# Values of later tokens through DRAM, memory slots last, and one attention store per segment, in a recurrent-memory attention kernel

## Chip, cores, metric

One core of one Trainium2 chip. The metric is device time in microseconds (us); lower is better. Before: median 1245.14 us (1236.84 to 1247.9, 4 runs).

## The reference

Attention in 64 segments of 32 tokens. Each segment attends over 8 memory slots and its own tokens; its output for the memory slots is the next segment's memory, so the segments form a chain. A gated feed-forward part follows.

```python
# S = 2048 tokens, Dm = 640, H = 32 heads of Dh = 128, M = 8 slots, seg_len = 32
for s in range(n_seg):
    h = concatenate([mem, x[:, 32 * s:32 * s + 32]], axis=1)          # 8 + 32 rows
    q, k, v = h @ Wq, h @ Wk, h @ Wv
    p = softmax(where(mask, q @ k.T * scale, -1e9))                   # token rows: causal; memory rows: all
    o = (p @ v) @ Wo
    mem = o[:, :M]                                                    # goes to the next segment
    outs.append(o[:, M:])
# then h = x + attention, and h + (relu(gate) * up) @ W_down on its layer norm
```

## The kernel before

TensorE projects 32 rows at a time: the 8 memory rows of segment s and, in the same pass, 24 *riders*, token rows that a later segment will need. Every fourth segment a group of 32 more tokens (`act_e`) is projected in between. The 32 heads lie in four groups g of 32 partitions: partition 32g + t holds row t of group g. The names in the profiles: `act_r` is the input of a pass; `tok` holds projected rows before their transpose; `Qr`, `KS` and `Kr` are the queries and keys that the scores read; `Vp` holds the values of the pass just projected, `Vr` those gathered for a segment's own tokens; `oT` is the attention output before the output projection, `wtok` the finished attention rows; `Pbd` holds the probabilities of the memory rows and, for `woe`, attention rows on their way out. Four features of this kernel matter here.

**1. A recorder derives all waits.** `add` notes what each operation reads and writes; a wait is made for each conflict of keys. All DMAs below are issued by SyncE, in program order: a DMA whose inputs aren't ready holds up all DMAs behind it (in the changed kernel's class 1 stretches, defined below, the inputs of KS are written by 9.9 us and KS is issued at 14.8, behind stores that wait; means of 14).

```python
def dma(dst, src, r=(), w=(), eng="sp"):
    add(eng, lambda e: e.dma_start(dst, src), r=r, w=w, dma=True)
```

**2. K goes through a DMA transpose every segment** (`KS<-tok`, and `Kr<-tok` for the 32 extra tokens of every fourth). The score matmuls wait for it.

```python
project(a, ks, 1, (0,), (P2,)); to_tok(P2, 0, "act")      # K, first half of the heads
project(a, ks, 1, (1,), (P3,)); to_tok(P3, 1, "dve")      # K, second half
dma_t(KS..., tokp[0][:, :], [("tok", 0), ("tok", 1)], [("KS",)])
# ... pv_x(s - 1), Q and V projections, evictions ...
scores(s)                                                 # reads KS, Kr, Qr
```

**3. The riders' values are moved by many small copies**, since tokens that sit at row 8 and up of their pass must sit at other rows in their own segment:

```python
def v_riders(par, t0, n):                                 # 4 or 8 copies of 8, 16 or 24 rows
    done = 0
    while done < n:
        t = t0 + done
        q, o = seg_slot(t // SEG), t % SEG
        m = min(n - done, SEG - o)
        for g in range(4):
            a = 32 * g + M + done
            dma(Vr[q][32 * g + o:32 * g + o + m, :, :], Vp[par][a:a + m, :, :], ...)
        done += m
```

**4. Attention rows are stored in four pieces a segment**, and the last 8 tokens of four segments, computed together (`woe`), in eight:

```python
def store_attn(src, skey, p0, t0, n):
    for g in range(4):
        dma(attn_d[t0:t0 + n, g, :], src[32 * g + p0:32 * g + p0 + n, :, :]..., r=[skey], w=[("attn", t0, g)])

def woe_store(b):                                         # where s % 4 == 1
    for j in range(4):
        for dg in range(2):
            t0 = 32 * (4 * b + j)
            dma(attn_d[t0:t0 + M, 2 * dg:2 * dg + 2, :]..., ap(Pbd, ...), r=[("Pbd", 0), ("Pbd", 1)], w=[("attn", t0, dg)])
# ... in the segment loop, after the scores: v_riders, pv_mem, wo_pass, store_attn, [Kr transpose], [woe_store]
```

The softmax here doesn't subtract the row's maximum and nothing guards it: scores larger than these inputs give would overflow.

## Time and profile before

I cut the trace at the first score matmul of each segment and call a segment's number modulo 4 its class: class 1 has the `woe` work and its stores, class 2 the Kr transpose. A stretch runs from the scores of one segment to those of the next, so what a class issues delays the scores at the end of its stretch.

| mean of 12 segments, us | class 0 | class 1 | class 2 | class 3 |
|---|---|---|---|---|
| length of the stretch | 14.69 | 16.43 | 16.01 | 15.74 |
| PE idle in it | 0.77 | 2.24 | 1.56 | 1.30 |

The loop from the second to the last scores takes 972.0 us, 94 of them with PE idle; the opening takes 38.7 and the feed-forward part 200.9 us.

Here are lines of the page of the kernel before: busy time by engine, then two groups (line, engine, operation, out<-in, count, busy us, mean ns, idle before it and what ended most of that).

```profile
PE 1114.9 (90%) x30140; PEld 577.0 (46%) x27792; DVE 564.4 (45%) x1438; ACT 333.2 (27%) x684; POOL 25.3 (2%) x92
...
L369 PE MATMUL ps<-ident,tok 128*128 128x128 bf16 x664 | 51.2, 220 | 17.9 <-DVE tok L378 13.3
...
L484 PE MATMUL ps<-Qr,Kr 128*32 128x40 bf16 x2048 | 41.9, 186 | 25.2 <-DMA KS<-tok 25.0
```

TensorE is the limit, but it stands 25.2 us before score matmuls, nearly all of it for the transpose of KS. The waits of the same kernel (who waited for whom: us in total, times, longest) show the second late transpose:

```profile
ACT tok L376 <- DMA Kr<-tok: 54.7, 12, 5.1
PE ps L484 <- DMA KS<-tok: 25.0, 16, 3.0
DVE tok L378 <- DMA Kr<-tok: 22.2, 12, 2.5
PE ps L369 <- DVE tok L378: 13.3, 11, 1.5
```

The Q evictions write the buffer that the Kr transpose reads, so they wait until it has landed, and PE's transposes of Q wait for them. Why the transposes are late is to be read from SyncE's timeline (start us, us, operation, out<-in, count), here a stretch of class 1 and the next of class 2:

```profile
636.28 6.34 SPq L306 DMA_DIRECT2D Vr<-Vp  x8
642.67 2.95 SPq L306 DMA_DIRECT2D attn_d<-wtok  x4
645.67 2.66 SPq L306 DMA_DIRECT2D attn_d<-Pbd  x8
648.43 1.26 SPq L309 DMA_TRANSPOSE KS<-tok  x1
...
652.78 5.72 SPq L306 DMA_DIRECT2D Vr<-Vp  x8
658.55 1.68 SPq L306 DMA_DIRECT2D attn_d<-wtok  x4
660.33 1.82 SPq L309 DMA_TRANSPOSE Kr<-tok  x1
```

The queue has no break: 12 us of issuing small copies, and only then KS, 3.6 us after its input was ready. In the mean SyncE issues for 14.2 of the 16.4 us of a class 1 stretch.

### The profile page before, as it was taken

The numbers are of one execution on the slowest core, as the hardware profiler recorded it, in microseconds if no ns is written. First come the engines' busy times: TensorE is split into PE (matmuls) and PEld (weight loads), VectorE is DVE, ScalarE is ACT, GpSimd is POOL, SyncE is SP. The second block draws the span as 40 slices with busy tenths as digits, with TensorE's granted clock in tenths as the row PEclk, the third lists the DMA queues.
The fourth block names the chain that finished last, engine by engine and source line by source line (L and its number), as shares of the span: only waits on it lengthen the run. The fifth ranks groups of instructions, "written<-read, shape, count | busy, mean of one in ns | idle before, by whom it ended". The sixth has DMA issues, their size and how long they took to land.

```text
span 1245.2 us, 62156 instructions
## 1 busy us (share of the span) xinstructions
PE 1114.9 (90%) x30140; PEld 577.0 (46%) x27792; DVE 564.4 (45%) x1438; ACT 333.2 (27%) x684; POOL 25.3 (2%) x92
## 2 busy tenths in 40 slices
PE   5589999989899989989988989999989986999998
PEld 2344445444445544544444544454445454533443
DVE  3244545444444444554544544454445442443522
ACT  2123223322232222232322222233223321211311
POOL 1000000000000000000000000000000000000000
PEclk9889999999999999999999999999999998999999
DMA  9933333324343334343434344423242329121200
GB/s 360 337 53 68 58 67 59 66 57 67 56 66 59 70 57 66 60 81 66 79 70 81 66 82 64 65 55 79 42 78 57 63 58 323 27 80 27 69 22 22
DMA packets 218274, 102.12 MB, mean 82 GB/s; under 512 B 190688, under 2 KB 206752, under 8 KB 218016
## 3 DMA queue, kind: packets, MB, share of 16 engines
q1 hardware_dynamic: 217824, 98.13, 36.8%
q8 instruction: 227, 3.72, 1.3%
q14 instruction: 31, 0.25, 0.1%
q10 hardware_dynamic: 192, 0.01, 0.0%
HBM read 36.79 MB, written 6.55 MB: 35 GB/s over the span
## 4 chain that ended last, share of the span: by engine, by line
PE 77%; DMA 11%; DVE 6%; SPq 3%; issue 3%; ACT 1%; DVEq 0%
PE ps L350 27%; PE ps L541 13%; PE ps L336 10%; PE ps L883 10%; DMA KS<-tok 5%; DMA Kr<-tok 3%; SPq L306 3%; PE ps L484 3%; PE ps L369 3%; PE ps L916 3%; PE ps L578 3%; PE ps L553 2%; DMA Wo<-in_A_Wo_dram 2%; PE ps L517 2%; DVE TBf L465 2%
## 5 line engine op out<-in xcount | busy, mean ns | idle before, releaser
L350 PE MATMUL ps<-W,act_r 128*32 128x512 bf16 x6640 | 456.5, 385 | 27.7 <-DVE act_r L466 12.7
L350 PEld LDWEIGHTS ps<-W,act_r 128*32 128x32 bf16 x6640 | 170.0, 97 | 275.4 <-issue 74.3
L541 PE MATMUL ps<-Wo,oT 128*32 128x160 bf16 x8448 | 165.3, 236 | 35.2 <-DVE oT L378 23.8
L378 DVE CAST tok<-ps 128x512 bf16<-128x512 f32 x161 | 111.1, 690 | 151.6 <-PE ps L350 97.3
L541 PEld LDWEIGHTS ps<-Wo,oT 128*32 128x32 bf16 x8448 | 149.1, 98 | 49.5 <-DVE oT L378 35.5
L376 ACT ACTIVATE tok<-ps 128x512 bf16<-128x512 f32 x161 | 95.9, 596 | 249.9 <-PE ps L336 134.6
L336 PE MATMUL ps<-W,act_r 128*32 128x512 bf16 x1240 | 120.6, 379 | 0.3 <-issue 0.3
L376 ACT ACTIVATE wtok<-ps 128x160 bf16<-128x160 f32 x64 | 19.5, 304 | 311.4 <-DVE TBf L465 302.3
L465 DVE STREAM_TRANSPOSE TBf<-ps 128x160 f32<-128x160 f32 x64 | 22.4, 350 | 174.6 <-PE ps L541 174.6
L350 PE MATMUL ps<-W,act_e 128*32 128x512 bf16 x900 | 94.2, 395 | 1.5 <-issue 1.5
L336 PE MATMUL ps<-W,act_e 128*32 128x512 bf16 x900 | 93.3, 392 | 0.8 <-issue 0.8
L591 DVE TENSOR_TENSOR ox<-ps,rx 128x512 bf16<-128x512 f32 x128 | 82.5, 686 | 2.2
L376 ACT ACTIVATE Qr<-ps 128x768 bf16<-128x768 bf16 (+3 forms) x110 | 69.2, 658 | 42.0 <-DVE Qr L378 26.7
L369 PE MATMUL ps<-ident,tok 128*128 128x128 bf16 x664 | 51.2, 220 | 17.9 <-DVE tok L378 13.3
L883 PE MATMUL ps<-xn2T,Wg 128*128 128x512 bf16 x260 | 65.6, 383 | 0.0
L883 PE MATMUL ps<-xn2T,Wu 128*128 128x512 bf16 x260 | 65.5, 383 | 0.0
L484 PE MATMUL ps<-Qr,Kr 128*32 128x40 bf16 x2048 | 41.9, 186 | 25.2 <-DMA KS<-tok 25.0
L898 DVE TENSOR_TENSOR hT<-g,ps 128x512 bf16<-128x512 bf16 (+1 forms) x56 | 38.5, 688 | 57.1 <-PE ps L883 53.3
L916 PE MATMUL ps<-Wd,hT 128*128 128x320 bf16 (+1 forms) x240 | 63.3, 300 | 0.0
L369 PEld LDWEIGHTS ps<-ident,tok 128*128 128x128 bf16 x664 | 37.4, 98 | 52.8 <-DVE tok L378 48.0
L378 DVE CAST Vp<-ps 128x512 bf16<-128x512 f32 x64 | 44.1, 689 | 33.1 <-PE ps L350 33.1
L896 ACT ACTIVATE g<-ps 128x512 bf16<-128x512 f32 (+1 forms) x56 | 32.5, 593 | 95.9 <-PE ps L883 95.9
(82 smaller groups left out, 1006.1 us busy)
## 6 DMA issues: line engine op xcount, KB each, us to landing
Vr<-Vp SPq DMA_DIRECT2D x124, 48.8 KB
W<-in_A_Wk_dram SPq DMA_DIRECT2D x2, 2560.0 KB
W<-in_A_Wq_dram SPq DMA_DIRECT2D x2, 2560.0 KB
W<-in_A_Wv_dram SPq DMA_DIRECT2D x2, 2560.0 KB
Wo<-in_A_Wo_dram SPq DMA_DIRECT2D x2, 2560.0 KB
xt<-in_A_x_dram SPq DMA_DIRECT2D x30, 160.0 KB
Vr<-Vp SPq DMA_DIRECT2D x128, 32.5 KB
attn_d<-wtok SPq DMA_DIRECT2D x256, 7.5 KB
```

Source lines behind the costliest of these rows:

```text
L336: return pe.add_instruction(mybir.InstMatmult(name=nc.get_next_instruction_name(), engine=mybir.EngineType.PE, ins=[pe.lower_ap(rhs), pe.l ...
L350: ins = pe.matmul(*a, start=(c == 0), stop=(c == DC - 1), skip_group_check=True)
L369: ins = pe.matmul(bank_bf(b)[:, k * 128:(k + 1) * 128], t[:, (k % 4) * 128:(k % 4 + 1) * 128], ident[:, :], is_transpose=True)
L376: add("act", lambda a: a.activation(dst, src, ACTF.Copy), r=r, w=w)
L378: add("dve", lambda v: v.tensor_copy(dst, src), r=r, w=w)
L465: add("dve", lambda v: v.transpose(TBf[:].rearrange("p c t -> p (c t)"), src), r=[wkey], w=[("TBf",)])
L484: i = pe.matmul(o, lh, Qr[:, h, q, :], start=True, stop=True, skip_group_check=True)
L541: i = pe.matmul(bank(bk)[32 * gg:32 * gg + 32, 0:160], src[:, hb, :], w[:, gg], start=(hb == 0), stop=(hb == 31), skip_group_check=True)
L591: add("dve", lambda v, kh=kh: v.tensor_tensor(ox[:, kh, :, :], src[:, :, kh, 0:128], ap(rx, kh, [[2, 4], [0, 128]]), ALU.mult), r=[B(b0 + ...
L883: ins = pe.matmul(bank(bk), w[:, c, lo:lo + 128], xn2T[par][:, c, :], start=(c == 0), stop=(c == DC - 1))
L898: add("dve", lambda v: v.tensor_tensor(hT[par][lo:128, j, :], g1[gi][lo:128, :], bank(bu)[lo:128, :], ALU.mult), r=[B(bu), ("g1", gi)], w= ...
L916: i = pe.matmul(*a, start=(j == 0), stop=(j == FC - 1), skip_group_check=True)
```

## The change

Intent: take most of those issues off SyncE. All rows of a pass are stored to a DRAM table by token number in one DMA (`v_store`), and the next segment's 32 rows come back in another (`v_load`); they can be whole tiles because the memory slots move to the end (rows 24 to 31), where a later store overwrites or a mask drops them. Attention rows go out in one store of all 32 rows. Its last 8 rows a segment are placeholders, so the two `woe` stores must land after it: a new dependence. The core of the diff (masks, row offsets and set-up cut):

```diff
+    v_d = nc.dram_tensor("v_d", [4, S + 32, 8 * VW], BF16)
...
-    def v_riders(par, t0, n):            # shown above: 4 or 8 copies
+    def v_rows(t0):
+        return bass.AP(v_d, t0 * 8 * VW, [[(S + 32) * 8 * VW, 4], [8 * VW, 32], [1, 8 * VW]])
+
+    def v_store(par, t0):
+        dma(v_rows(t0), Vp[par][:].rearrange("p k d -> p (k d)"), r=[("Vp", par), ("Vp1", par)], w=[("v_d",)])
+
+    def v_load(s):
+        dma(Vr[s % 2][:].rearrange("p k d -> p (k d)"), v_rows(SEG * s), r=[("v_d",)], w=[("Vr", s % 2)])
...
-    def store_attn(src, skey, p0, t0, n):
-        for g in range(4):
-            dma(attn_d[t0:t0 + n, g, :], src[32 * g + p0:32 * g + p0 + n, :, :]..., r=[skey], w=[("attn", t0, g)])
+    def store_attn(src, skey, s):
+        dma(bass.AP(attn_d, SEG * s * D, [[160, 4], [D, SEG], [1, 160]]), src[:]..., r=[skey], w=[("attn", s)])
...
     def woe_store(b):
-        for j in range(4):
-            for dg in range(2):
-                ...
+        for dg in range(2):
+            dma(bass.AP(attn_d, (128 * b + RID) * D + 320 * dg, [[SEG * D, 4], [D, M], [1, 320]]),
+                ap(Pbd, 0, [[1, 320]], 32 * dg, 32), r=[("Pbd", 0), ("Pbd", 1)] + [("attn", 4 * b + j) for j in range(4)],
+                w=[("attne", b, dg)])
...
         if s > 0 and nr:
-            v_riders(par, t0, nr)
+            v_store(par, t0)
...
         to_act(s + 1, B(T1), bank(T1)[:, 0:160])
+        if s > 0 and (s + 1) % 4 != 1:
+            v_load(s + 1)
         if s >= 2:
             wo_rows(T1, wtok[par], ("wtok", par), "act")
-            store_attn(wtok[par], ("wtok", par), M, 32 * (s - 2) + M, RID)
+            store_attn(wtok[par], ("wtok", par), s - 2)
```

Also: the mask (`min`) on the probabilities Px now covers both halves, 512 instead of 256 elements a row, and the K weights of the score matmuls for the memory half have 32 columns instead of 8.

More of the change, by code (lines that the diff above doesn't have):

```diff
@@ L221, in build_kernel @@
     mbd = ar.alloc("mbd", [128, 2, 32], BF16)
-    mca = ar.alloc("mca", [128, SEG], BF16)
+    mca = ar.alloc("mca", [128, 2, SEG], BF16)
     act_r = [ar.alloc(f"act_r{i}", [128, 4, DC, 32], BF16) for i in range(2)]
@@ L229, in build_kernel @@
     Qr = ar.alloc("Qr", [128, H, RING // SEG, M + SEG], BF16)
-    Vr = [ar.alloc(f"Vr{i}", [128, 8, VW], BF16) for i in range(RING // SEG)]
+    Vr = [ar.alloc(f"Vr{i}", [128, 8, VW], BF16) for i in range(2)]
     Vp = [ar.alloc(f"Vp{i}", [128, 8, VW], BF16) for i in range(2)]
@@ L281, in build_kernel @@
     for g in range(4):
-        add("pool", lambda p, g=g: p.affine_select(mca[32 * g:32 * g + 32, :], mca[32 * g:32 * g + 32, :], [[1, SEG]],
-                                                   ALU.is_ge, 0.0, base=0, channel_multiplier=-1),
-            r=[("mca",)], w=[("mca",)])
+        for a in range(2):
+            add("pool", lambda p, g=g, a=a: p.affine_select(mca[32 * g:32 * g + 32, a, :], mca[32 * g:32 * g + 32, a, :],
+                                                            [[1 - a, SEG]], ALU.is_ge, 0.0, base=-RID * a,
+                                                            channel_multiplier=2 * a - 1), r=[("mca",)], w=[("mca",)])
     add("dve", lambda v: v.memset(mbd[:], 0.0), w=[("mbd",)])
@@ L287, in build_kernel @@
         add("dve", lambda v, g=g: v.memset(mbd[32 * g:32 * g + 32, 0, 8 * g:8 * g + 8], BIG), r=[("mbd",)], w=[("mbd",)])
-        add("dve", lambda v, g=g: v.memset(mbd[32 * g:32 * g + M, 1, 8 * g:8 * g + 8], BIG), r=[("mbd",)], w=[("mbd",)])
-    add("dve", lambda v: v.memset(bank(P1), 0.0), w=[B(P1)])
+        add("dve", lambda v, g=g: v.memset(mbd[32 * g:32 * g + 32, 1, 8 * g:8 * g + 8], BIG), r=[("mbd",)], w=[("mbd",)])
+        add("pool", lambda p, g=g: p.affine_select(mbd[32 * g:32 * g + 32, 1, :], mbd[32 * g:32 * g + 32, 1, :], [[0, 32]],
+                                                   ALU.is_ge, 0.0, base=-RID, channel_multiplier=1),
+            r=[("mbd",)], w=[("mbd",)])
     for i in range(2):
@@ L295, in build_kernel @@
         add("pool", lambda p, i=i: p.memset(ap(Vp[i], Dh, [[VW, 8], [1, VW - Dh]]), 1.0), w=[("Vp1", i)])
-    for i in range(RING // SEG):
-        add("pool", lambda p, i=i: p.memset(ap(Vr[i], Dh, [[VW, 8], [1, 1]]), 1.0), w=[("Vr1", i)])
+        add("pool", lambda p, i=i: p.memset(ap(Vr[i], Dh, [[VW, 8], [1, VW - Dh]]), 1.0), w=[("Vr", i)])
     def table(a):
@@ L402, in seg_slot @@
         return (s - 2) % (RING // SEG)
-    def v_riders(par, t0, n):
-        done = 0
-        while done < n:
-            t = t0 + done
-            q, o = seg_slot(t // SEG), t % SEG
-            m = min(n - done, SEG - o)
-            for g in range(4):
-                a = 32 * g + M + done
-                dma(Vr[q][32 * g + o:32 * g + o + m, :, :], Vp[par][a:a + m, :, :], r=[("Vp", par), ("Vp1", par), ("Vr1", q)],
-                    w=[("Vr", q, g, o)])
-            done += m
-    def vr_keys(q):
-        return [("Vr", q)] + [("Vr1", q)] + [("Vr", q, g, o) for g in range(4) for o in (0, 8, 16, 24)]
+    def v_rows(t0):
[4 more added lines that the diff above has]
+        dma(Vr[s % 2][:].rearrange("p k d -> p (k d)"), v_rows(SEG * s), r=[("v_d",)], w=[("Vr", s % 2)])
     def n_rows(b):
@@ L444, in ln1_back @@
         for j in range(full):
-            copy(act_r[b % 2][:, j, :, M:32], src[:, :, RID * j:RID * (j + 1)], [("act", b % 2, "x", j)])
+            copy(act_r[b % 2][:, j, :, 0:RID], src[:, :, RID * j:RID * (j + 1)], [("act", b % 2, "x", j)])
         if n == 128:
@@ L448, in ln1_back @@
         elif n % RID:
-            copy(act_r[b % 2][:, full, :, M:M + n % RID], src[:, :, RID * full:n], [("act", b % 2, "x", full)])
+            copy(act_r[b % 2][:, full, :, 0:n % RID], src[:, :, RID * full:n], [("act", b % 2, "x", full)])
     def chunks_of(flat):
@@ L465, in to_act @@
         add("dve", lambda v: v.transpose(TBf[:].rearrange("p c t -> p (c t)"), src), r=[wkey], w=[("TBf",)])
-        add("dve", lambda v: v.tensor_copy(act_r[b % 2][:, j, :, 0:M], TBf[:, :, 0:M]), r=[("TBf",)],
+        add("dve", lambda v: v.tensor_copy(act_r[b % 2][:, j, :, RID:32], TBf[:, :, RID:32]), r=[("TBf",)],
             w=[("act", b % 2, j, "m")])
@@ L482, in f @@
                         else:
-                            o, lh = bank(P1)[32 * g:32 * g + M, 40 * k:40 * k + 40], KS[:, h, 0:M]
+                            o, lh = bank(P1)[32 * g:32 * g + 32, 40 * k:40 * k + 40], KS[:, h, :]
                         i = pe.matmul(o, lh, Qr[:, h, q, :], start=True, stop=True, skip_group_check=True)
@@ L503, in exp_x @@
                                           ACTF.Exp, scale=SCALE), r=[B(P0), B(P1)], w=[("Px",)])
-        add("dve", lambda v: v.tensor_tensor(ap(Px, 0, [[32, 8], [1, 32]]), ap(Px, 0, [[32, 8], [1, 32]]),
-                                             ap(mca, 0, [[0, 8], [1, 32]]), ALU.min), r=[("Px",), ("mca",)],
+        add("dve", lambda v: v.tensor_tensor(ap(Px, 0, [[256, 2], [32, 8], [1, 32]]), ap(Px, 0, [[256, 2], [32, 8], [1, 32]]),
+                                             ap(mca, 0, [[32, 2], [0, 8], [1, 32]]), ALU.min), r=[("Px",), ("mca",)],
             w=[("Px",)])
     def pv_mem(s):
-        q = seg_slot(s)
         par = s % 2
@@ L512, in f @@
             def f(pe, a=a):
-                t = Vr[q] if a == 0 else Vp[par]
+                t = Vr[par] if a == 0 else Vp[par]
                 for hf in range(2):
@@ L519, in f @@
                 return i
-            add("pe", f, r=[("Pbd", a)] + ([("Vp", par), ("Vp1", par)] if a else vr_keys(q)), w=[B(T1)])
+            add("pe", f, r=[("Pbd", a)] + ([("Vp", par), ("Vp1", par)] if a else [("Vr", par)]), w=[B(T1)])
         src = bank(T1)[:, 0:258].rearrange("p (a d) -> p a d", d=129)
@@ L531, in trans_om @@
         add("pe", f, r=[("om",), ("ident",)], w=[B(T1)])
-        copy_op("dve", ap(oT[s % 2], 0, [[16 * SEG, 2], [SEG, 4], [4 * SEG, 4], [1, M]]),
+        copy_op("dve", ap(oT[s % 2], RID, [[16 * SEG, 2], [SEG, 4], [4 * SEG, 4], [1, M]]),
                 bank_bf(T1)[:, 0:256].rearrange("p (a j g q) -> p a j g q", a=2, j=4, g=4), [B(T1)], [("oT", s % 2, "m")])
@@ L560, in wo_rows @@
         copy_op(eng, dst[:].rearrange("p c j -> p (c j)"), bank(bk)[:, 0:160], [B(bk)], [dkey])
-    def store_attn(src, skey, p0, t0, n):
-        for g in range(4):
-            dma(attn_d[t0:t0 + n, g, :], src[32 * g + p0:32 * g + p0 + n, :, :].rearrange("p c j -> p (c j)"),
-                r=[skey], w=[("attn", t0, g)])
+    def store_attn(src, skey, s):
+        dma(bass.AP(attn_d, SEG * s * D, [[160, 4], [D, SEG], [1, 160]]), src[:].rearrange("p c j -> p (c j)"), r=[skey],
+            w=[("attn", s)])
     def pv_x(s, b0):
-        q = seg_slot(s)
         par = s % 2
@@ L576, in f @@
                         for g in range(4):
-                            n, t = (32, Vr[q]) if a == 0 else (M, Vp[par])
+                            t = Vr[par] if a == 0 else Vp[par]
                             i = pe.matmul(bank(b0 + g)[32 * c:32 * c + 32, 129 * kh:129 * kh + 129],
-                                          Px[32 * g:32 * g + n, 256 * a + 32 * k:256 * a + 32 * k + 32],
-                                          t[32 * g:32 * g + n, k, 0:129], start=(a == 0), stop=(a == 1),
+                                          Px[32 * g:32 * g + 32, 256 * a + 32 * k:256 * a + 32 * k + 32],
+                                          t[32 * g:32 * g + 32, k, 0:129], start=(a == 0), stop=(a == 1),
                                           skip_group_check=True, tile_position=(32 * g, 32 * c))
             return i
-        add("pe", f, r=[("Px",), ("Vp", par), ("Vp1", par)] + vr_keys(q), w=[B(b0 + g) for g in range(4)])
+        add("pe", f, r=[("Px",), ("Vp", par), ("Vp1", par), ("Vr", par)], w=[B(b0 + g) for g in range(4)])
     def norm_x(b0):
@@ L600, in copy_oTe @@
         o = M * (s % 4)
-        copy_op("dve", oTe[:, :, o:o + M], oT[s % 2][:, :, 0:M], [("oT", s % 2, "m")], [("oTe", s % 4)])
+        copy_op("dve", oTe[:, :, o:o + M], oT[s % 2][:, :, RID:32], [("oT", s % 2, "m")], [("oTe", s % 4)])
     def attn_keys(i):
-        ks = []
-        for s in range(4 * i, 4 * i + 4):
-            ks += [("attn", 32 * s + M, g) for g in range(4)] + [("attn", 32 * s, g) for g in range(2)]
-        return ks
+        return [("attn", s) for s in range(4 * i, 4 * i + 4)] + [("attne", i, dg) for dg in range(2)]
     def add_attn(h, x, a, r, w):
@@ L638, in build_kernel @@
     for g in range(4):
-        dma(wtok[1][32 * g:32 * g + M, :, :],
+        dma(wtok[1][32 * g + RID:32 * g + 32, :, :],
             mem0_ap.rearrange("t (c g j) -> g t c j", g=4, j=32)[g], r=[("wtok", 1)], w=[("wtok0", g)], eng="act")
@@ L678, in opening_back @@
         if j == 1:
-            copy_op("dve", KS[:, :, 0:M], slots(bk, 0, M), [B(bk)], [("KS",)])
-            evac_k(slots(bk, 0, SEG), B(bk), 64, RID, M, "act")
-        else:
-            copy_op("dve", Qr[:, :, q, 0:M], slots(bk, 0, M), [B(bk)], [("Qm", q)])
-            evac_q(bk, 64, RID, M, "act")
+            copy_op("dve", KS[:, :, :], slots(bk, 0, SEG), [B(bk)], [("KS",)])
+            evac_k(slots(bk, 0, SEG), B(bk), 64, RID, 0, "act")
+        else:
+            copy_op("dve", Qr[:, :, q, 0:M], slots(bk, RID, SEG), [B(bk)], [("Qm", q)])
+            evac_q(bk, 64, RID, 0, "act")
     for j in (1, 0):
@@ L704, in build_kernel @@
         for n, (a, ks) in enumerate(groups):
-            q = seg_slot(n - 1)
-            t, key = (Vr[q], ("Vr", q)) if n else (Vp[0], ("Vp", 0))
+            t, key = (Vr[n - 1], ("Vr", n - 1)) if n else (Vp[0], ("Vp", 0))
             project(a, ks, 2, (i,), vbanks[n][i:i + 1])
             to_v(vbanks[n][i], t, i, key, ("act", "dve")[(i + n) % 2])
-    v_riders(0, 64, RID)
+    v_store(0, 64)
     def load_gate_up():
@@ L743, in evac @@
                 if j == 2:
-                    to_v(BQ[i], Vr[q], i, ("Vr", q), e)
+                    to_v(BQ[i], Vr[(s + 1) % 2], i, ("Vr", (s + 1) % 2), e)
                 else:
@@ L765, in woe_store @@
     def woe_store(b):
-        for j in range(4):
-            for dg in range(2):
-                t0 = 32 * (4 * b + j)
-                dma(attn_d[t0:t0 + M, 2 * dg:2 * dg + 2, :].rearrange("t g f -> t (g f)"),
-                    ap(Pbd, 0, [[1, 320]], 32 * dg + M * j, M), r=[("Pbd", 0), ("Pbd", 1)], w=[("attn", t0, dg)])
+        for dg in range(2):
+            dma(bass.AP(attn_d, (128 * b + RID) * D + 320 * dg, [[SEG * D, 4], [D, M], [1, 320]]),
+                ap(Pbd, 0, [[1, 320]], 32 * dg, 32), r=[("Pbd", 0), ("Pbd", 1)] + [("attn", 4 * b + j) for j in range(4)],
+                w=[("attne", b, dg)])
     fin = None
@@ L814, in build_kernel @@
                 trans8(tok[2], ("tok", 2), tok[3], ("tok", 3), P3)
-                copy_op("dve", Qr[:, :, q, 0:M], slots(P3, 0, M), [B(P3)], [("Qm", q)])
+                copy_op("dve", Qr[:, :, q, 0:M], slots(P3, RID, SEG), [B(P3)], [("Qm", q)])
             if nr:
-                evac_k(KS, ("KS",), t0, nr, M, "dve")
-                evac_q(P3, t0, nr, M, "act")
+                evac_k(KS, ("KS",), t0, nr, 0, "dve")
+                evac_q(P3, t0, nr, 0, "act")
             if s % 4 == 2 and ln:
@@ L941, in rows @@
         wo_rows(bk, wtok[p], ("wtok", p), "act")
-        store_attn(wtok[p], ("wtok", p), M, 32 * s + M, RID)
+        store_attn(wtok[p], ("wtok", p), s)
     copy_oTe(s - 1)
```

## The prediction

> **What bounds the kernel now.** TensorE. The page gives PE busy 1114.9 of 1245.2 us (90%); 972 us are the recurrent segments, 15 to 16 us each. Between first and last score matmuls of that loop PE is idle for 94 us. Much of it is fixed hand-overs (waits for the oT copy 23.8, the act_r copy 12.7 us). The removable part stands in the view of waits: score matmuls waiting for the DMA transpose of KS, 25.0 us in 16 waits; transposes of tok waiting for an eviction (PE 13.3 us) that itself waits for the DMA transpose of Kr (ACT 54.7, DVE 22.2).
>
> **Why those are late.** SyncE issues in order. In the timeline, eight Vr copies take 5.7 to 6.3 us to issue, four attn stores 1.7 to 3.0, and every fourth segment eight Pbd stores 2.7; then comes KS. At 636 to 648 us KS is issued 3.6 us after its tok is ready, and PE stands 2.0 us. By segment number modulo 4, KS is issued 0.0, 1.5, 1.1, 0.0 us late (means); Kr 0.6. All PE waits for KS fall in classes 1 and 2.
>
> **What the change removes, adds, moves.**
> - DMAs on SyncE: 376 Vr copies become 63 stores and 47 loads; 256 attn stores 64; 128 Pbd stores 32. At 0.3 to 0.7 us each (medians of issue duration) that frees several us a segment; the late issues vanish. The queue now waits for the v store to land, and the Pbd stores for the attn stores; both should be over before KS.
> - Bytes: 12 MB of Vr copies become about 29 MB through DRAM. [...] 24-row copies show 12+1 landings, 8-row ones 8+1. The new copies have slowest dimension 4: four engines, 32 packets of 2080 B each. At 0.08 to 0.13 us a packet (trace) I estimate 2.6 to 4.3 us plus about 1.5. So the store lands about 5, the load about 10 us after the scores start. Kr, issued at 8.5, may queue a little behind the load; KS, at 10 to 11, hardly.
> - VectorE: the min on Px goes from 256 to 512 elements a row. It takes 297 ns; f32 results of 256 and 512 (424, 686 ns) show a fixed 0.16 us, so I estimate 0.43. It ends 1.84 us after scores start, rm starts at 1.96 to 2.0: nearly hidden, 2 us in all.
> - PE: same matmuls; KS weights have 32 columns instead of 8. Both kinds of score matmuls start at equal intervals, so no cost.
>
> **On the critical path.** Gain: KS waits 22 to 25 us, tok waits behind Kr about 5, stray ones 1 to 2: about 30. Given back: Px 2, DMA contention 0 to 8. Net about 26 us.
>
> Predicted 1218 us, 8 in 10 within 1203 to 1235. Faster by over 2%: 0.50; within 2%: 0.46; slower: 0.04.
>
> **Right if** PE idle in the loop falls from 94 to about 65 us, waits of scores for KS fall below 5 us, KS is issued within 0.2 us of tok in all classes, PE busy stays near 1115 us, Px min near 0.43 us. **Wrong if** the v store lands later than about 8 us, so that the queue stands there and delays attn stores and Kr; if the four-engine copies stretch the transposes' 3.5 to 4 us to landing; if another wait stands just behind (oT, act_r, VectorE); or if the wider KS weights slow the scores.

The forecast's sum: about 30 us gained, 2 and 0 to 8 given back, net about 26, from 1245 to 1219 us. "Four engines" was the author's assumption: no copy of the new shape had run. The changed kernel shows it (4 + 1 landing steps, see below). The 1.5 us beside the packets was the author's estimate too; in the trace before, the first packet of a row of Vr copies starts 1.4 us after the issue (median of 63 rows).

## The result, and the profile after

Changed kernel: median 1320.4 us (1318.01 to 1323.56, 4 runs), before 1245.14. The ratio is 1.0618 (95% interval 1.0559 to 1.0676): 6% slower. Ratios here are the mean time of one kernel's fast runs over that of the other's of the same rounds, so not quite the ratio of the medians that I quote. For attn_first, spread16, attn_half and the two "whole" runs below, the difference from before is clear of the noise, but its interval leaves open whether it is over 2%. All outputs are right.

The page of the changed kernel, the lines that answer to those of before:

```profile
PE 1132.8 (86%) x30140; PEld 586.1 (45%) x27792; DVE 573.4 (44%) x1437; ACT 332.9 (25%) x684; POOL 27.0 (2%) x99
...
L481 PE MATMUL ps<-Qr,Kr 128*32 128x40 bf16 x2048 | 42.6, 188 | 61.7 <-DMA KS<-tok 61.7
...
L372 PE MATMUL ps<-ident,tok 128*128 128x128 bf16 x664 | 52.4, 223 | 32.7 <-DVE tok L381 26.6
```

The very waits that were to go have more than doubled for KS (25.2 to 61.7 us) and nearly doubled for tok. By class, the stretches are 14.66, 18.18, 17.92 and 16.10 us: class 0 is as before, class 1 has lost 1.75 us, class 2 1.9, class 3 0.36. The loop takes 1043.2 us (71 more), with PE idle for 147; the opening (38.8) and the feed-forward part (201.9) are as they were.

SyncE issues far less now, but stands. The waits of its queue in the changed kernel that before had no counterpart:

```profile
SPq L309 <- DMA v_d<-Vp: 262.7, 47, 9.0
...
SPq L121 <- DMA attn_d<-wtok: 79.9, 16, 5.4
```

47 times the queue waits for the v store to land before it may issue the load, 5.6 us each; 16 times, in class 1, it waits 5.0 us for the attn store. The timeline of SyncE in the changed kernel, again a class 1 stretch and the following one of class 2:

```profile
602.73 0.52 SPq L309 DMA_DIRECT2D v_d<-Vp  x1
608.79 0.55 SPq L309 DMA_DIRECT2D Vr<-v_d  x1
609.38 0.53 SPq L309 DMA_DIRECT2D attn_d<-wtok  x1
615.39 1.29 SPq L309 DMA_DIRECT2D attn_d<-Pbd  x2
616.78 1.25 SPq L312 DMA_TRANSPOSE KS<-tok  x1
...
621.16 0.53 SPq L309 DMA_DIRECT2D v_d<-Vp  x1
627.20 0.54 SPq L309 DMA_DIRECT2D Vr<-v_d  x1
628.26 0.55 SPq L309 DMA_DIRECT2D attn_d<-wtok  x1
628.90 1.49 SPq L312 DMA_TRANSPOSE Kr<-tok  x1
```

Read the starts, not the durations: 6 us pass between store and load, 6 us between the attn store and the Pbd stores that wait for it. The chain that ended last, in the class 1 stretch (start us, us, what), runs through exactly this:

```profile
614.57 0.57 PE ps L372 x8
615.14 0.02 issue
615.16 0.30 DVE Qr L381
615.47 0.56 SPq L309
616.02 0.04 issue
616.07 0.61 SPq L309
616.68 0.06 issue
616.74 0.02 SPq L121
616.75 0.03 issue
616.78 3.29 DMA KS<-tok
620.08 0.14 issue
620.21 0.66 PE ps L481 x64
```

The two `SPq L309` are the Pbd stores: KS stands behind them, and PE waits 3.89 us for KS before 620.21. (The page names DVE as what released the first of them; SyncE's own waits name the attn store, and its landing at 615.3 agrees. A wait for several things is put down to one.)

The landings in the trace put numbers on each step. Means of 14 segments a class. I read the number of engines of a copy from its landing steps, and "on k engines" stands for that from here on: in the kernel before, Vr copies of 24 rows show 12 + 1, of 16 rows 16, of 8 rows 8 + 1; in the changed kernel every v store and v load shows 4 + 1. For the four the trace of the changed kernel has a second sign: the times of a v store's 128 packets add up to 3.7 times the stretch from the first one's start to the last one's end (a load's to 3.8), and while a store moves (604.5 to 607.5 us) the DMA share is 0.26 of the 16 engines, while a load does (610.5 to 613.5 us) 0.24. "At" is us after the start of the stretch; the load, attn, Kr and KS columns are for the classes named.

| | steps | v store: to landing | v load: at, landed at | attn store, class 1: to landing | Kr: at, to landing | KS, class 1: at, landed at |
|---|---|---|---|---|---|---|
| before | 12 or 8 + 1 (Vr), 12 + 1 (attn) | (Vr copies: 2.4) | | 1.90 | 9.05, 4.09 | 12.36, 16.14 |
| changed | 4 + 1 (v and attn) | 6.03 | 6.97, 12.77 | 5.74 | 8.57, 6.33 | 14.76, 18.02 |

In class 0, which has no v load, the same attn store lands in 2.36 us. Behind the load it lands 0.5 us after the load does (13.29 against 12.77).

### The profile page after: what moved, and what is told of

Its sections match the earlier page's. It is cut to its first block, busy times and chain, and to the rows that moved or that the text cites. A ratio compares the mean times of both kernels' runs of the same rounds, so it can differ in the third digit from the quotient of the medians.

```text
span 1316.5 us, 61419 instructions
## 1 busy us (share of the span) xinstructions
PE 1132.8 (86%) x30140; PEld 586.1 (45%) x27792; DVE 573.4 (44%) x1437; ACT 332.9 (25%) x684; POOL 27.0 (2%) x99
## 4 chain that ended last, share of the span: by engine, by line
PE 70%; DMA 17%; DVE 6%; SPq 4%; issue 3%; ACT 1%; DVEq 0%
PE ps L353 24%; PE ps L537 12%; PE ps L339 9%; PE ps L875 9%; DMA Kr<-tok 6%; DMA KS<-tok 5%; SPq L309 4%; PE ps L372 3%; PE ps L481 3%; PE ps L908 3%; PE ps L573 2%; DMA Wo<-in_A_Wo_dram 2%; PE ps L549 2%; DMA v_d<-Vp 2%; PE ps L513 2%
## 5 line engine op out<-in xcount | busy, mean ns | idle before, releaser
L537 PEld LDWEIGHTS ps<-Wo,oT 128*32 128x32 bf16 x8448 | 152.4, 99 | 50.8 <-DVE oT L381 35.3
L353 PE MATMUL ps<-W,act_e 128*32 128x512 bf16 x900 | 101.7, 421 | 2.2 <-issue 2.2
L339 PE MATMUL ps<-W,act_e 128*32 128x512 bf16 x900 | 102.0, 422 | 0.7 <-issue 0.7
L481 PE MATMUL ps<-Qr,Kr 128*32 128x40 bf16 x2048 | 42.6, 188 | 61.7 <-DMA KS<-tok 61.7
L481 PEld LDWEIGHTS ps<-Qr,Kr 128*32 128x32 bf16 x2048 | 39.2, 96 | 77.6 <-issue 64.5
```

What stands on the lines that cost most here:

```text
L339: return pe.add_instruction(mybir.InstMatmult(name=nc.get_next_instruction_name(), engine=mybir.EngineType.PE, ins=[pe.lower_ap(rhs), pe.l ...
L353: ins = pe.matmul(*a, start=(c == 0), stop=(c == DC - 1), skip_group_check=True)
L481: i = pe.matmul(o, lh, Qr[:, h, q, :], start=True, stop=True, skip_group_check=True)
L537: i = pe.matmul(bank(bk)[32 * gg:32 * gg + 32, 0:160], src[:, hb, :], w[:, gg], start=(hb == 0), stop=(hb == 31), skip_group_check=True)
```

## The experiments

**Theory A.** The new copies run on four DMA engines. Each takes about 6 us, and what comes later and needs the same engines, or stands later in SyncE's queue, waits: attn, Pbd, KS in class 1; Kr in class 2. Rivals: **B**, the way through DRAM is slow as such; **C**, the new dependence of the Pbd stores on the attn stores alone is guilty. Formed on the way: **D**, many copies are simply quicker than one; **E**, the clock of TensorE adds to the loss; **F**, store and load one after the other are what costs.

### spread16: each v copy in four, on 16 engines

```diff
-        dma(v_rows(t0), Vp[par][:]..., w=[("v_d",)])                      # 4 x 32 rows
+        for i in range(4):                                                # 32 rows each, one group
+            dma(v_rows(t0, i), Vp[par][32 * i:32 * i + 32]..., w=[("v_d", i)])
```

The load likewise; part i of the load waits for part i of the store.

> Edit: the changed kernel, but each v store and each v load is issued as four copies of 32 rows (one for each group of partitions), so that the slowest dimension is 32 and, [...] 16 engines work on each instead of 4. Same bytes, same way through DRAM, same order. Theory A (four engines: each v copy takes 6 us, and the attn store, Kr and KS queue behind it on the same engines): the v store lands in under 3.5 us instead of 6.0, the v load likewise, the attn store in about 2.4 instead of 5.7, Kr in about 4.2 instead of 6.3, PE's wait for KS in class 1 falls from 3.45 us to under 1, and the time is 1205 to 1240 us. Rival B (the way through DRAM itself, and its bytes): the v copies still take 5 us or more and the time stays above 1290. Rival C (only the new dependence of the Pbd stores on the attn stores): class 1 improves only as far as the attn store lands earlier, Kr stays at 6 us, time about 1265.

Measured: 1208.09 us against 1234.73, ratio 0.9773 (0.9733 to 0.9813). Landings show 16 steps. The four parts of the store have all landed 3.8 us after the first issue, the load has landed at 7.8 instead of 12.8 us, the attn store of class 1 lands in 2.30 us, Kr in 3.80; KS of class 1 is issued at 10.56. PE is idle for 64 us in the loop. SyncE's timeline in spread16, one class 1 stretch:

```profile
609.50 2.49 SPq L309 DMA_DIRECT2D v_d<-Vp  x4
612.26 1.70 SPq L309 DMA_DIRECT2D Vr<-v_d  x4
615.04 0.53 SPq L309 DMA_DIRECT2D attn_d<-wtok  x1
617.36 1.27 SPq L309 DMA_DIRECT2D attn_d<-Pbd  x2
618.74 1.25 SPq L312 DMA_TRANSPOSE KS<-tok  x1
```

and its waits of PE for KS:

```profile
PE ps L491 <- DMA KS<-tok: 8.0, 4, 6.3
```

B falls: the same bytes still go through DRAM, and the kernel is faster than before by 2.3%. But this edit alters three things at once (engines, number of copies, finer waits); shape4 and the two "whole" runs take them apart.

### attn_first: the attn store ahead of the load

```diff
-        if s > 0 and (s + 1) % 4 != 1:
-            v_load(s + 1)
         if s >= 2:
             wo_rows(...); store_attn(...)
+        if s > 0 and (s + 1) % 4 != 1:
+            v_load(s + 1)
```

> Edit: the changed kernel with one swap in the order of issue: the attn store stands before the v load. It then no longer queues behind the load, but the load still runs on four engines. Theory A: the attn store lands about 2 to 3 us after issue, the Pbd stores wait no more, the class 1 gap before the scores falls from 3.45 us to under 1 and with it most of the 19 half-clock windows in the loop; Kr and KS of class 2 still land in about 6 and 5 us behind the load. Time 1250 to 1275 us. Rival B: class 1 is late because the queue stands at the v store, so a swap behind that point gains little: above 1300. Rival C: as A in class 1, but class 2 was never slow because of the load, so nothing of it is left to gain.

Measured: 1255.0 us against 1234.73, ratio 1.0172. Swapping two issues takes back 4.5 of the 6.2 points. The attn store of class 1 lands in 2.28 us, KS is issued at 10.38. Kr is as slow as before the swap (6.45 us), and the waits of attn_first show that the loss left sits there:

```profile
PE ps L372 <- DVE tok L381: 30.6, 15, 3.4
...
PE ps L481 <- DMA KS<-tok: 10.3, 5, 7.6
```

So A holds in both classes: class 1 was the attn store behind the load, class 2 is Kr behind the load.

### v_half and attn_half: each half of the change alone

v_half keeps the v copies of the change and stores attention rows as before (four stores of 24 rows, eight Pbd stores, no dependence). attn_half is the kernel before with the attention stores of the change:

```diff
-    def store_attn(src, skey, p0, t0, n):
-        for g in range(4):
-            dma(attn_d[t0:t0 + n, g, :], src[32 * g + p0:32 * g + p0 + n, :, :]..., w=[("attn", t0, g)])
+    def store_attn(src, skey, s):
+        dma(bass.AP(attn_d, SEG * s * D, [[160, 4], [D, SEG], [1, 160]]), src[:]..., w=[("attn", s)])
# and two Pbd stores that wait for the attn stores, at row 128 * b
```

> Edit: only the v half of the change: v through DRAM on four engines and memory slots last, but attention rows stored as before (four stores of 24 rows a segment, eight Pbd stores, no dependence between them). Theory A: v store and load still 6 us; nothing waits for the attn stores, so the large class 1 gap goes, but SyncE issues 12 more copies there, so KS stays about 1 us late; Kr still lands in about 6 us. Time 1255 to 1290. Rival C: the whole loss is gone, 1245 or below. Rival B: the whole loss stays, 1310 or above.

> Edit: only the attention half of the change on the kernel before: one attn store of 32 rows a segment, two Pbd stores that wait for the attn stores, Vr copies as before, memory slots first. Theory A: with no four-engine v load ahead of it the attn store lands in about 2.4 us, so the dependence costs nothing and the saved issues bring KS a little forward: 1225 to 1242. Rival C: the dependence alone delays KS by 2 us or more in class 1: 1270 or more.

Measured, against 1234.73: v_half 1264.67, ratio 1.0252; attn_half 1207.03, ratio 0.9770 (0.9735 to 0.9806). The attention half alone is as good as spread16, and better than I had expected: with 288 fewer attn and Pbd issues in all (nine fewer in a class 1 stretch), KS of class 1 is issued at 10.91 instead of 12.36 and Kr at 7.72 instead of 9.05, which brings PE's waits for KS from 25.0 to 9.1 us, and those of its transposes of tok from 13.3 to 3.6:

```profile
PE ps L484 <- DMA KS<-tok: 9.1, 7, 3.7
```

The dependence costs next to nothing here, though the queue does wait (28.0 us in 16 waits in attn_half, 1.75 us each; the Pbd stores go out at 9.8 us, when KS is not yet ready): C falls. v_half fell into its range, but not quite as told: with three more issues ahead of it than in the changed kernel (attention rows in four stores instead of one) Kr was issued at 9.9 us instead of 8.6 and then landed in 3.9, late by its issue and not by its transfer. The halves don't add: 0.977 times 1.025 is about 1.00, and together they gave 1.062. The surplus is their meeting (attn_first, above, shows it by one swap): the attn store made *necessary for progress* by one half was put *behind a 6 us copy* by the other.

### shape4: four copies, but on four engines

```diff
-  [[8 * VW, 32], [1, 8 * VW]]                                     # DRAM side of one part, in spread16
+  [[64 * VW + PAD, 4], [8 * VW, 8], [1, 8 * VW]]                  # a pad of 64 elements after every 8 rows
```

> Edit: the kernel spread16 with one thing altered: the DRAM rows get a small pad after every 8 rows, so that each of the four copies is described as 4x8 rows instead of 32. Number of copies, rows, bytes, order and result are those of spread16; only the slowest dimension goes from 32 back to 4. Theory A (number of engines): landings show 4+1 steps again, the v store takes about 6 us until its last part lands and the load as well, Kr lands in about 6 us, and the time goes back to 1290 to 1350 us. Rival D (spread16 was fast because four small copies pipeline better than one large one): time stays at 1205 to 1225.

Measured: 1225.66 us against 1236.37, ratio 0.9916 (0.9881 to 0.9952). Landings show 4 + 1 steps where spread16 shows 16, so the shape did set the number of landing steps, and so of engines as read from them. But the time didn't go back to 1290: A as I had put it fails here, and D, which had said 1205 to 1225, was nearly met. Only 1.4 points separate four engines from sixteen (0.9916 from spread16's 0.9773). The four-engine parts have landed 4.7 us after the first issue, and the load ends at 9.4, not 12.8 us, because each of its parts starts as soon as its own part of the store is there (first issue at 3.5 instead of 7.0 us). So the loss isn't in the number of engines alone; it needed more.

### load16 and store16: only one of the two spread

```diff
# load16: v_store as in the changed kernel (one copy), v_load as in spread16; store16 the other way round
```

> Edit: only the v load is issued as four copies on 16 engines; the v store stays one copy on four. Theory A, the share of the load: with the store alone slow the queue stands until 7 us after the scores, the load lands before 10.5, attn about 11, Kr again in about 4 us; the Pbd stores wait a little, so class 1 keeps a gap of 0.5 to 1.5 us. Time 1212 to 1238.

> Edit: only the v store is issued as four copies on 16 engines; the v load stays one copy on four. Theory A, the share of the store: the load is issued at about 4 us and lands at about 10 us after the scores; the attn store, issued at 6.8, still lands behind it at about 10.5; Kr, issued at 7.6, lands in about 4.5 to 5. Class 1 gap 0.5 to 1.5 us. Time 1212 to 1245.

Measured, against 1236.37: load16 1255.14, ratio 1.0141; store16 1245.18, ratio 1.0066. Both miss, load16 clearly. In load16 the queue stands as long as in the changed kernel:

```profile
SPq L309 <- DMA v_d<-Vp: 262.7, 47, 9.3
```

and then needs four issues for the load instead of one, so the attn store is issued at 9.1 us (class 1) and Kr at 9.6 instead of 8.6. In store16 the load starts at 4.8 us and lands at 10.2; the attn store lands at 10.8 and Kr takes 5.3 us. I had counted the time on the engines and not the time for which the queue stands. Both are worse than shape4, which uses four engines throughout: whole copies wait for whole copies there.

### shape4_whole and spread16_whole: the finer waits taken away

```diff
-            dma(v_part(Vr[s % 2], i), v_rows(SEG * s, i), r=[("v_d", i)], ...)
+            dma(v_part(Vr[s % 2], i), v_rows(SEG * s, i), r=[("v_d", k) for k in range(NV)], ...)
```

> Edit: shape4 (four copies for the store and four for the load, each on four engines), but every part of the load waits for all four parts of the store instead of its own part. Theory F (the store and the load one after the other are what costs: the issuing queue stands until the whole store has landed, and the attn store and Kr come behind the load): the load starts at about 6 us instead of 3.5 after the scores and ends at about 11.5 instead of 9.4, the attn store is issued at 8 and lands at about 12, Kr is issued about 1 us later, the class 1 gap is 2 us or more; time 1250 to 1285, against 1226 for shape4. Rival D (several copies are simply quicker than one, whatever their order): within 8 us of shape4.

> Edit: the same coarser wait in spread16 (16 engines). Theory F: the store is whole at about 4.9 us, so the load starts at 5 instead of 3.3 and ends at about 8.8 instead of 7.8, still before the attn store and Kr suffer much: 1208 to 1222, against 1208 for spread16. So with 16 engines the coarse wait costs under half of what it costs with four.

Measured, against 1244.29: shape4_whole 1275.63, ratio 1.0244; spread16_whole 1223.5, ratio 0.9841 (its ratio is worth quoting rather than its time: the runs of before in this call were 0.8% slower than in the first). The one wait costs 3.3 points on four engines and 0.7 on sixteen (the two intervals overlap there, so the 0.7 is hardly clear of noise). In shape4_whole the load is issued from 5.7 us on and has landed at 11.7, the attn store of class 1 lands at 12.4 and KS is issued at 13.8. F holds, D in its simple form falls: more copies without the overlap leave the kernel 2.4% slower than before. Yet D isn't empty: four parts alone, on the same four engines and with the coarse wait, take back 3.7 of the 6.2 points; the store has landed 1.3 us sooner there (5.7 instead of 7.0) and the load 1.1. Nor is the number of engines always small: with the coarse wait sixteen instead of four are worth 4.0 points, with the finer one 1.4. The five kernels side by side:

| | ratio to before | load landed at | attn store, class 1, landed at |
|---|---|---|---|
| changed: one store, one load, four engines | 1.0618 | 12.8 | 13.3 |
| shape4_whole: four parts, four engines, coarse wait | 1.0244 | 11.7 | 12.4 |
| shape4: the same, each part waits for its own | 0.9916 | 9.4 | 10.1 |
| spread16_whole: four parts, 16 engines, coarse wait | 0.9841 | 8.9 | 9.6 |
| spread16: the same, each part waits for its own | 0.9773 | 7.8 | 9.1 |

In these five the time follows the end of the load. What the Pbd stores and KS can bear shows in the last column: KS is ready to go at 10 to 11 us, and the two Pbd issues need about 1.3 before it.

### kept_busy and both_busy: is it the clock?

From the third scores on, the changed kernel's trace shows half clock (the granted TensorE clock at 0.5) in 19 windows, 84 us of the loop, instead of 5 (17 us) before, and PE's busy time is 18 us longer. Of the 19 windows 18 begin within 1.8 us of the end of a single PE gap of 2.2 to 3.9 us; before, three of the five begin within 1 us of the end of a gap of 2.0 to 2.3 us. So theory E: the clock costs part of the loss. Useless matmuls fill the gaps (their output is overwritten; in both_busy 14 of them keep PE busy for 3.0 us, 10 for 2.1):

```diff
+            if s % 4 == 2 and s < 60:      # kept_busy: before the scores; both_busy: also 10 before the transposes of Q where s % 4 == 3
+                for _ in range(14):
+                    pe.matmul(bank(P0)[:, :], ident[:, :], Wo[:, 0, 0:512], start=True, stop=True, ...)
```

> Edit: the changed kernel with 14 useless matmuls of 512 columns (about 3 us) before the scores of every fourth segment, where TensorE otherwise stands idle for 3.45 us; they write a bank that the scores overwrite, so the result is right. The gap itself isn't shortened. Theory E (beside the gaps, the half clock that follows each long gap costs about 1.1 us in each of 16 places): half-clock windows in the loop fall from 19 to under 9, time 1297 to 1310 us. Without that theory: 1318 to 1325.

> Edit: kept_busy, and 10 more useless matmuls (2.2 us) before the transposes of tok in the following segment, where TensorE stood 2.5 us for Kr in that run and where its half-clock windows had moved. Results stay right. Theory E (half clock costs 15 to 20 us of the loss, and moved from one gap to the next in kept_busy): half-clock windows in the loop fall from 15 to under 6 and the time to 1298 to 1308 us. If the clock isn't worth that, or the useless matmuls delay useful ones: 1312 to 1325.

Measured: kept_busy 1316.33 against 1236.37, ratio 1.0640; both_busy 1322.19 against 1244.29, ratio 1.0630. The changed kernel has 1.0618. In kept_busy 15 windows are left: they moved from the end of class 1 stretches to the end of class 2 stretches. In both_busy all but 2 are gone (16 us of the loop), and the mean granted clock is 0.982 instead of 0.960, as these answers for the changed kernel and for both_busy say:

```profile
core 0: 1316.5 us, clock 0.960
```

```profile
core 0: 1319.4 us, clock 0.982
```

Same time at a better clock: E, with its 15 to 20 us, falls. It doesn't exclude a cost of some us, since the useless matmuls held up useful ones here and there: in the changed kernel the scores of class 2 begin 0.14 us after KS has landed and the transposes of tok 0.84 us after Kr, nearly everywhere; in both_busy these delays add up to some 6 us more. That the matmuls at half speed ran in time which the next late transpose would have taken anyway is my reading and fits this; no run shows it apart.

## Why the prediction was wrong

**What bounds the kernel: right.** KS and Kr were late because SyncE was busy issuing. attn_half and spread16 both take that away and run at 0.977 of before, 27 us less, with PE idle for 66 and 64 us in the loop. The prediction's gain was "about 30", its net "about 26 us" and its idle time "about 65". What it didn't see is that fewer attention stores alone bring all of that, and that sending the values through DRAM, even on sixteen engines, adds nothing to it.

**VectorE and PE: right.** The Px min takes 426 ns (predicted 430), as this line of the changed kernel's groups shows; the score matmuls with 32 weight columns take 187 ns (180 with 8). With the same VectorE and PE work spread16 gains in full.

```profile
L501 DVE TENSOR_TENSOR Px<-Px,mca 128x512 bf16<-128x512 bf16 x64 | 27.2, 426 | 9.6 <-ACT Px L499 9.6
```

**Four engines: right (4 + 1 landing steps), but too quick.** The store was to land at about 5 us and the load at about 10; they landed at 7.0 and 12.8 (classes 1 to 3). The packets of the store took 0.127 us in the mean (median 0.085), so at the slow end of my 0.08 to 0.13. My estimate for one copy was 4.1 to 5.8 us; the store took 6.0 and the load 5.8. Of the store's 6.0, 1.2 pass before the first packet starts and 0.5 after the last one ends (medians of 63 stores), near the 1.5 I had put. The "about 5" and "about 10" left only some 4 us for the store, the bottom of that range, and 5 for the load, and the two stand in series. The range itself was low: in the trace of the kernel before, packets of this size took 0.142 us in the mean (median 0.131), and 32 of these plus 1.5 would have given 6.0.

**The step that failed** is this one: "The queue now waits for the v store to land, and the Pbd stores for the attn stores; both should be over before KS." I looked at each wait alone. The Pbd stores wait for an attn store that stands behind the load on the same four engines, and the load behind the store in the queue: 1.0 us until the store is issued, 6.0 until it lands, 5.8 until the load lands, 0.5 until the attn store does. That is 13.3 us, and the two Pbd issues, and only then KS, at 14.8 us instead of 12.4. The first half of the sentence held (the store landed at 7.0, before KS was ready), the second didn't. attn_first shows this link by one swap (1.0618 to 1.0172), attn_half shows that without the v copies the wait is harmless.

**The term that was mis-sized** is "DMA contention 0 to 8": between the changed kernel (1.0618) and attn_half (0.977), which has the gain and none of the v copies, lie 8.5 points, about 105 us. "Kr ... may queue a little behind the load" was 2.2 us more to landing (4.09 to 6.33); issued 0.5 us earlier, Kr landed 1.8 us later, and the class 2 stretch grew by 1.9. "KS ... hardly" was 1.0 and 1.4 us more to landing in classes 2 and 3 (5.0 and 5.2, where it had taken 3.9 to 4.0). The prediction's own "Wrong if" list had the right suspects: it named a late store, a stretched transpose and delayed attn stores, with 8 us as the bound for the store. The store landed at 7 us, inside that bound, and it went wrong all the same, because the bound was for one link and not for the chain.

**What stays open.** Why one copy of 128 rows on four engines takes 6.0 us when four copies of 32 rows, also on four engines, are done 4.7 us after the first issue: the packets of the single copy take 0.127 us on average against 0.094, and the long ones stand at its start; no run here says why. That the attn store and the load share the *same* four engines is inferred from the landing steps and from who waits for whom; the trace doesn't name the engine of a packet. How the saving would split if the Pbd stores' dependence were removed from the changed kernel and nothing else was not run; v_half comes near (no dependence, 1.0252), but issues nine more stores in a class 1 stretch.

## What to carry to other kernels

Fewer DMA issues are no gain where something behind them in the same queue waits for a landing that comes too late: follow the whole chain (store lands, load issued, load lands, next store lands, its reader issued) and compare its end with the moment when the critical transfer must be issued (here 13.3 us after the scores, in class 1, where the inputs of KS were there at 9.9). Look at the outermost dimension of a merged copy, and see whether it can be described so that it isn't small (here a dimension of 4 showed 4 + 1 landing steps and one of 32 showed 16, and sixteen engines instead of four were worth 1.4 to 4.0 points); a copy in parts, each with its own wait, lets the way back start early (in shape4 at 3.5 instead of 7.0 us). And where two changes come together, run each alone: here one half held the whole gain.
